# Block sums of the values on TensorE, and the low words of the weights rounded by ScalarE

## The chip, the core and the metric

One core of one Trainium2 chip runs the whole program. The engines named here are PE (TensorE, matrix multiply; PEld is its weight load), DVE (VectorE), ACT (ScalarE), POOL (GpSimd) and SP (SyncE, which issues every DMA of this kernel). The metric is the device time of one execution in microseconds (us); lower is better.

## The reference

A local-plus-summary attention over 2 batches, 8 heads, 768 positions and 64 channels is followed by two feed-forward layers on 1536 tokens of 512 channels. Weights and inputs of the layers arrive as float64, the attention's as float32.

```python
block, window = (32, 16)
nb = S // block                                   # 24 blocks
k_sum = k.reshape(B, H, nb, block, D).max(axis=3)
v_sum = v.reshape(B, H, nb, block, D).mean(axis=3)
scores_l = where(|i - j| < window, scale * q @ k.T, -1e9)
scores_s = scale * q @ k_sum.T + log(block)
a = softmax(concat([scores_l, scores_s]))
x = a @ concat([v, v_sum])                        # -> 1536 x 512
x = (x @ w_a) * (x @ w_b) @ w_out                 # d_ff = 1536
h = x @ w_in                                      # d_ff = 2048
return maximum(0.01 * h, h) @ w_out2
```

What matters here is `v_sum`, the mean of every 32 rows of v, and the conversion of the float64 weights.

## The kernel before

**Feed-forward part.** All products of the two layers run as three float32r matmuls of 512 columns (high times high, high times rest, rest times high; `mm3`, L578 to L582). A unit is a slice `s` of four hidden columns blocks and a chunk `c` of 512 tokens; `first_product` (L661) makes `x @ w_a` and `x @ w_b` into the PSUM banks a, b, c0, c1, `y_products` (L698) the product with `w_out`; the second layer follows at L783 to L798.

**Weights.** The chip has no float64, so each 128 x 512 piece arrives as pairs of 32-bit words (`wst`, two buffers) and is converted by seven steps in `convert` (L321): `low` (L335) scales the low word by 2^-29 and rounds it to an integer (DVE, L337) and takes the absolute value of the high word (ACT, L341); `clamp`, `shift`, `join` and `add` (L345 to L362, DVE) build the float32 bits; `high` (ACT, L367) and `rest_of` (DVE, L370) write the two parts in `wsp`, which the matmuls read. The buffer of the rounded low word, `wr`, is single. There are 68 such pieces in all. The steps stand in the list `bg`, from which `tick` takes a few after each product, so that they are spread between other work.

**Attention part.** `attention_ops` (L202) gives each step of the attention a place number: 8 per pair of blocks of 256 queries (`pairs`, twelve of them), plus an offset, and the list is sorted by it. The first four pairs run before the first unit of the feed-forward part, with the first matmuls of that part among them; the others are spread over the units (0, 0) and (0, 1) by `micro`. The steps share four PSUM banks t0 to t3 in turn (`at_bank`): keys are transposed and reduced by maximum (`k_prep`), queries transposed (`q_prep`), scores made in 64 x 64 quarters of the PE array (L515), masked and exponentiated (L528 on DVE, L532 on ACT), normalised, transposed, and multiplied with windows of v (`pv`, L562).

**Block sums of v.** Once for each batch `load_vb` (L149) brings v as three tiles `vb` of 128 half blocks x 16 rows x 64 channels. `v_sums` (L424) puts six DVE reductions (L428) at the head of `bg`: each sums the 16 rows of one tile for 32 channels. `v_place` (L440) then adds the two halves of every block, scales by 1/32 and moves each head's 24 blocks to partitions 0 to 23 by ten matmuls of 64 columns with the matrix `place` (L452); ACT copies the result (L459) and POOL spreads it over the windows (`put_sums`, L191).

The order on each engine's queue is worked out at compile time from the order of the code and a planner's estimate of the durations, so that instructions can stand elsewhere than the code has them.

Of the kernel before, what the change touches and what calls it, by code (L numbers as in the profile page):

```python
# [11 lines left out]
F32 = mybir.dt.float32  # L12
F32R = mybir.dt.float32r
I32 = mybir.dt.int32
U32 = mybir.dt.uint32
AF = mybir.ActivationFunctionType
ALU = mybir.AluOpType
AX = mybir.AxisListType
# [3 lines left out]
def kernel(  # L22
# [12 lines left out]
    nc = tc.nc  # L35
    B, H, S, D = q.shape
    P = 128
    BLK = 32
    WIN = 16
    NB = S // BLK  # L40
# [16 lines left out]
    T = 512  # L57
# [13 lines left out]
    const = ctx.enter_context(tc.tile_pool(name="const", bufs=1))  # L71
# [10 lines left out]
    sm_p = att.enter_context(tc.tile_pool(name="sm", bufs=4))  # L82
    at_p = att.enter_context(tc.tile_pool(name="at", bufs=2))

    def bank(tag):
        return psum.tile([P, T], F32, tag=tag, name=f"ps_{tag}")
# [5 lines left out]
    def at_bank():  # L92
        cnt["at"] += 1
        return bank(at_banks[cnt["at"] % len(at_banks)])
# [26 lines left out]
    NV = 2 * H * NB // P  # L121
    vb_tiles = [xp.tile([P, BLK // 2, D], F32, tag="x", name=f"vb{j}") for j in range(NV)]
    vs_t = {}
    bg, vb_done = [], [None]

    pace = {"micro": 0.0, "bg": 3, "after": None}
    q_t, k_t, vb_t, vw_of = {}, {}, {}, {}
# [19 lines left out]
        q_t[i] = t  # L147

    def load_vb(b):  # L149
        while vb_done[0] in bg:  # L150
            bg.pop(0)()
        src = v[b].rearrange("h (n j) d -> (h n) j d", j=BLK // 2)
        for i, t in enumerate(vb_tiles):
            nc.sync.dma_start(out=t, in_=src[i * P : (i + 1) * P])
# [43 lines left out]
    LOAD, SIDE, PRODUCT = range(3)  # L198
# [3 lines left out]
    def attention_ops():  # L202

        ops = []
        seen = set()
        for i, p in enumerate(sum(pairs, [])):

            def add(at, kind, f, *args):
                ops.append((PER * i + at, kind, lambda: f(*args), i))

            for m, (b, hp) in enumerate(dict.fromkeys(x[:2] for x in p)):
                if (b, hp) not in seen:
                    seen.add((b, hp))
                    add(-18, LOAD, load_k, b, hp)
                    for j in range(2):
                        add(2 * m + j - 12, PRODUCT, k_prep, b, hp, j)
                    if hp == 0:
                        add(-5, LOAD, load_vb, b)
                        add(-4, SIDE, v_sums, b)
                        add(7, PRODUCT, v_place, b)  # L220
            add(-14, LOAD, load_q, i, p)
            add(-6, PRODUCT, q_prep, i, p)
            for j in range(2):
                add(4 * j, PRODUCT, scores, i, p, j)
                add(4 * j + 3, SIDE, normal, i, j)
                add(4 * j + 8, PRODUCT, p_transpose, i, j)
            add(1, LOAD, load_vw, i, p)
            add(9, SIDE, put_sums, i, p)
            add(PV, PRODUCT, pv, i, p)
        ops.sort(key=lambda o: o[:2])  # L230
        return ops
# [5 lines left out]
    ident = const.tile([P, P], F32, tag="ident", name="ident")  # L237
# [9 lines left out]
    t = negm[1]  # L247
# [3 lines left out]
    for c in range(2):  # L251
        for o, c0, c1 in ((0, 0, W), (W, SC, P)):
# [3 lines left out]
                out=loc, in_=loc, compare_op=ALU.is_ge, fill=BIG,  # L256
# [3 lines left out]
                out=loc, in_=loc, compare_op=ALU.is_ge, fill=BIG,  # L260
# [4 lines left out]
        nc.vector.memset(negm[i][:, c0 : c0 + WIN], BIG)  # L265
    for t in vw_t:
        nc.gpsimd.memset(t, 0.0)

    V0 = 32
    place = const.tile([P, P], F32, tag="place", name="place")  # L270
    nc.gpsimd.memset(place, 1.0 / BLK)
    for base, pattern, mult in ((2 * V0, [[-2, P]], 1), (1 - 2 * V0, [[2, P]], -1)):

        nc.gpsimd.affine_select(
            out=place, in_=place, compare_op=ALU.is_ge, fill=0.0,
# [29 lines left out]
    def stage():  # L305
        key = pieces[cnt["st"]]
        cnt["st"] += 1
        nm, f = key
        t = wst_p.tile([P, 1024], I32, tag="wst", name="wst")
        if nm in "op":  # L310
            src = {"o": w_o, "p": w_o2}[nm][P * f : P * (f + 1), :]
            nc.sync.dma_start(out=t, in_=src)
        else:
            src = {"a": w_a, "b": w_b, "i": w_i}[nm][:, 2 * P * f : 2 * P * (f + 1)]
            nc.sync.dma_start(
                out=t.rearrange("p (k f) -> p k f", k=KT),
                in_=src.rearrange("(k p) f -> p k f", p=P),
            )
        staged[key] = t

    def convert():  # L321

        i = cnt["conv"]
        key = pieces[i]
        while cnt["st"] < min(i + 4, len(pieces)):
            stage()
        cnt["conv"] += 1
        ww = staged.pop(key).rearrange("p (f two) -> p f two", two=2)
        lo_w, hi_w = ww[:, :, 0], ww[:, :, 1]
        home = "early" if room["early"] else "late"  # L330
        assert room[home], key
        room[home] -= 1
        t = {}

        def low():  # L335
            t["r"] = wcv_p.tile([P, 512], I32, tag="wr", name="wr", bufs=1)
            nc.vector.tensor_scalar(  # L337
                out=t["r"], in0=lo_w.bitcast(U32), scalar1=2.0**-29, scalar2=None, op0=ALU.mult
            )
            t["c"] = wcv_p.tile([P, 512], I32, tag="wc", name="wc")  # L340
            nc.scalar.activation(out=t["c"].bitcast(F32), in_=hi_w.bitcast(F32), func=AF.Abs)  # L341

        def clamp():
            c = t["c"].bitcast(F32)
            nc.vector.tensor_scalar(  # L345
                out=c, in0=c, scalar1=F_LO, scalar2=F_HI, op0=ALU.max, op1=ALU.min
            )

        def shift():
            nc.vector.tensor_scalar(  # L350
                out=t["c"], in0=t["c"], scalar1=3, scalar2=0x3FFFFFF8,
                op0=ALU.logical_shift_left, op1=ALU.bitwise_and,
            )

        def join():
            nc.vector.scalar_tensor_tensor(  # L356
                out=t["c"], in0=hi_w, scalar=-0x40000000, in1=t["c"],
                op0=ALU.bitwise_and, op1=ALU.bitwise_or,
            )

        def add():
            nc.vector.tensor_tensor(out=t["c"], in0=t["c"], in1=t["r"], op=ALU.add)  # L362

        def high():
            pool = wsp_p if home == "early" else late["wsp"]
            t["w"] = pool.tile([P, 2, 512], F32R, tag="wsp", name="wsp")
            nc.scalar.copy(out=t["w"][:, 0], in_=t["c"].bitcast(F32))  # L367

        def rest_of():
            nc.vector.tensor_tensor(  # L370
                out=t["w"][:, 1], in0=t["c"].bitcast(F32), in1=t["w"][:, 0].bitcast(F32),
                op=ALU.subtract,
            )
            w_of[key] = t["w"], home

        bg.extend([low, clamp, shift, join, add, high, rest_of])

    def may_convert():
# [42 lines left out]
            xt[c, kt] = xp.tile([P, 2, T], F32R, tag="x", name=f"x{c}_{kt}")  # L421
        return xt[c, kt]

    def v_sums(b):  # L424

        v0 = sm_p.tile([P, NV, D], F32, tag="v0", name="v0", bufs=1)
        ops = [
            lambda i=i, d=d: nc.vector.tensor_reduce(  # L428
                out=v0[:, i, d : d + D // 2],
                in_=vb_tiles[i][:, :, d : d + D // 2].rearrange("p j d -> p d j"),  # L430
                op=ALU.add, axis=AX.X,
            )
            for i in range(NV)
            for d in (0, D // 2)
        ]
        bg[0:0] = ops
        vb_done[0] = ops[-1]
        vb_t[b] = v0, ops[-1]

    def v_place(b):  # L440

        v0, done = vb_t.pop(b)
        while done in bg:
            bg.pop(0)()
        ps = at_bank()
        for h in range(H):
            r0, r1 = 2 * h * NB, 2 * (h + 1) * NB
            tiles = range(r0 // P, (r1 - 1) // P + 1)
            for i in tiles:
                c0 = V0 + (r0 - i * P) // 2  # L450
                assert 0 <= c0 <= P - NB
                nc.tensor.matmul(  # L452
                    out=ps[0:NB, h * D : (h + 1) * D],
                    lhsT=place[:, c0 : c0 + NB],
                    rhs=v0[:, i],
                    start=i == tiles[0], stop=i == tiles[-1],
                )
        vs = sm_p.tile([NB, H, D], F32, tag="vs", name="vs", bufs=2)
        nc.scalar.copy(out=vs, in_=ps[0:NB].rearrange("p (h d) -> p h d", h=H))  # L459
        vs_t[b] = vs  # L460
# [167 lines left out]
    ops = attention_ops()  # L628
# [32 lines left out]
    def first_product(key, src, c):  # L661

        w = weights(key)
        ps = product_bank(key[0])
        for kt in range(KT):
            kt_mm(ps, w, src[c, kt], kt)
            if kt == KT // 2 - 1:
                interleave()
        return ps
# [114 lines left out]
    for f, c in slices2:  # L784
        ps = first_product(("i", f), ysp, c)
        h = g_p.tile([P, T], F32, tag="g", name="h")
        nc.scalar.copy(out=h, in_=ps)  # L787
        nc.vector.scalar_tensor_tensor(  # L788
            out=h, in0=h, scalar=0.01, in1=ps, op0=ALU.mult, op1=ALU.max
# [41 lines left out]
```

## Time and profile before

| | us |
|---|---|
| median of three runs (lowest, highest) | 661.57 (661.22, 662.78) |
| the profiled execution, own time | 661.62 |
| its span on the core | 659.9 |
| PE busy in the span | 635.6 (96%) |
| DVE busy | 422.0 (64%) |
| ACT busy | 267.8 (41%) |

The span runs from the first to the last instruction that the profiler saw; 1.7 us of the profiled execution lie around it. Busy shares are averages over stages with different limits, and the ends of matmuls are modelled, so a PE that is shown busy is not always a PE at its peak. The page also cuts the span in 40 slices of 16.5 us and gives the clock that was granted to PE in each.

### The profile page before, as it was taken

To read this page: it belongs to the slowest core of one execution; us is meant where nothing else is said; L and a number is where in the kernel's file an instruction comes from. 1 tells how busy PE (TensorE), PEld (TensorE's weight loads), DVE (VectorE), ACT (ScalarE), POOL (GpSimd) and SP (SyncE) were. 2 spreads that over 40 slices of the span, in tenths; PEclk is the share of its full clock that TensorE was granted. 3 is DMA by queue.
4 is the path that set the end of the run, shared out by engine and by line. 5 is a ranking of instruction groups with operands and counts; after the bars stand their busy time and mean duration, and the time that the engine had idled before them with its cause. 6 is when DMAs were issued, how large, how long until landed. Compare 5 with 4: busy or idle time off the path is not lost.

```text
span 659.9 us, 9321 instructions
## 1 busy us (share of the span) xinstructions
PE 635.6 (96%) x3448; PEld 518.4 (79%) x3448; DVE 422.0 (64%) x968; ACT 267.8 (41%) x607; POOL 21.1 (3%) x38
## 2 busy tenths in 40 slices
PE   5699799999999999999999999999999999999997
PEld 4567577777888888888888888888888888888886
DVE  5989999955999972699623779732279532422323
ACT  4677386653445421344222535322255322222221
POOL 3210020000000000000000000000000000000000
PEclk9899799999999999999999999999999999999999
DMA  9976543512334430143200232400014000100101
GB/s 239 258 174 162 148 107 109 151 26 65 125 130 133 156 96 1 64 125 121 74 1 0 67 93 77 147 1 1 0 51 141 1 0 1 64 1 1 64 1 64
DMA packets 72590, 53.43 MB, mean 81 GB/s; under 512 B 46176, under 2 KB 66656, under 8 KB 72544
## 3 DMA queue, kind: packets, MB, share of 16 engines
q1 hardware_dynamic: 72544, 52.84, 27.0%
q8 instruction: 27, 0.44, 0.3%
q14 instruction: 19, 0.16, 0.1%
HBM read 49.68 MB, written 3.15 MB: 80 GB/s over the span
## 4 chain that ended last, share of the span: by engine, by line
PE 89%; DVE 7%; ACT 2%; DMA 1%; issue 1%; SPq 0%; DVEq 0%; ACTq 0%
PE ps_t L580 38%; PE ps_c L580 19%; PE ps_a L580 14%; PE ps_b L580 13%; PE ps_t L515 2%; DVE pm L528 1%; PE ps_t L550 1%; PE ps_t L562 1%; ACT pm L532 1%; DVE v L428 1%; DVE pm L542 1%; DMA wst<-in_moe_w_b_dram 1%; DVE wc L356 1%; PE ps_t L497 1%; DVE wr L337 0%
## 5 line engine op out<-in xcount | busy, mean ns | idle before, releaser
L580 PE MATMUL ps_t<-x,wsp 128*128 128x512 f32 x336 | 78.6, 389 | 0.0
L580 PE MATMUL ps_c<-wsp,gs 128*128 128x512 f32 x288 | 75.8, 389 | 0.0
L580 PE MATMUL ps_t<-wsp,gs 128*128 128x512 f32 x288 | 74.7, 389 | 0.0
L580 PEld LDWEIGHTS ps_t<-x,wsp 128*128 128x128 f32 x336 | 63.1, 188 | 13.1
L580 PE MATMUL ps_t<-ys,wsp 128*128 128x512 f32 x288 | 71.9, 389 | 0.0
L580 PE MATMUL ps_a<-x,wsp 128*128 128x512 f32 x252 | 68.6, 410 | 3.0 <-DVE wsp L370 2.7
L341 ACT ACTIVATE wc<-wst 128x512 f32<-128x512 f32 x68 | 45.6, 673 | 55.3 <-DMA wst<-in_moe_w_out_dram 12.1
L580 PE MATMUL ps_b<-x,wsp 128*128 128x512 f32 x252 | 64.3, 394 | 0.5 <-DVE wsp L370 0.5
L580 PEld LDWEIGHTS ps_t<-ys,wsp 128*128 128x128 f32 x288 | 54.1, 188 | 11.2
L580 PEld LDWEIGHTS ps_c<-wsp,gs 128*128 128x128 f32 x288 | 54.0, 188 | 11.2
L580 PEld LDWEIGHTS ps_t<-wsp,gs 128*128 128x128 f32 x288 | 54.0, 188 | 11.2
L580 PE MATMUL ps_c<-gs,wsp 128*128 128x512 f32 x240 | 60.8, 394 | 0.0
L580 PEld LDWEIGHTS ps_a<-x,wsp 128*128 128x128 f32 x252 | 47.9, 194 | 14.2 <-DVE wsp L370 3.1
L788 DVE SCALAR_TENSOR_TENSOR h<-h,ps_t 128x512 f32<-128x512 f32 x24 | 16.5, 686 | 60.8 <-ACT h L787 60.8
L580 PEld LDWEIGHTS ps_b<-x,wsp 128*128 128x128 f32 x252 | 46.6, 188 | 10.6 <-DVE wsp L370 1.0
L370 DVE TENSOR_TENSOR wsp<-wc,wsp 128x512 fp32r<-128x512 f32 x68 | 47.2, 696 | 9.9 <-ACT wsp L367 9.8
L580 PEld LDWEIGHTS ps_c<-gs,wsp 128*128 128x128 f32 x240 | 44.4, 188 | 9.5 <-ACT x L572 0.2
L367 ACT CAST wsp<-wc 128x512 fp32r<-128x512 f32 x68 | 42.1, 622 | 19.6 <-DVE wc L362 13.8
L580 PE MATMUL ps_t<-gs,wsp 128*128 128x512 f32 x192 | 47.7, 390 | 0.0
L601 DVE TENSOR_TENSOR gs<-h,gs 128x512 fp32r<-128x512 f32 x48 | 33.1, 691 | 22.8 <-ACT gs L600 22.7
L362 DVE CUSTOM_DVE_ANT_0 wc<-wc,wr 128x1024 uint16<-128x1024 uint16 x68 | 46.6, 685 | 0.6
L356 DVE SCALAR_TENSOR_TENSOR wc<-wst,wc 128x512 int32<-128x512 int32 x68 | 46.7, 689 | 0.2
(86 smaller groups left out, 835.9 us busy)
## 6 DMA issues: line engine op xcount, KB each, us to landing
wst<-in_moe_w_out_dram SPq DMA_DIRECT2D x28, 512.0 KB, 3.3
wst<-in_moe_w_in_dram SPq DMA_DIRECT2D x16, 512.0 KB, 3.7
wst<-in_moe_w_a_dram SPq DMA_DIRECT2D x12, 512.0 KB, 3.6
wst<-in_moe_w_b_dram SPq DMA_DIRECT2D x12, 512.0 KB, 3.6
k<-in_k_dram SPq DMA_DIRECT2D x16, 192.0 KB, 3.5
vb<-in_v_dram SPq DMA_DIRECT2D x6, 512.0 KB, 5.3
out_dram<-acc SPq DMA_DIRECT2D x12, 256.0 KB, 2.1
q<-in_q_dram SPq DMA_DIRECT2D x16, 128.0 KB, 2.9
```

Source lines behind the costliest of these rows:

```text
L341: nc.scalar.activation(out=t["c"].bitcast(F32), in_=hi_w.bitcast(F32), func=AF.Abs)
L356: nc.vector.scalar_tensor_tensor(out=t["c"], in0=hi_w, scalar=-0x40000000, in1=t["c"], op0=ALU.bitwise_and, op1=ALU.bitwise_or,)
L362: nc.vector.tensor_tensor(out=t["c"], in0=t["c"], in1=t["r"], op=ALU.add)
L367: nc.scalar.copy(out=t["w"][:, 0], in_=t["c"].bitcast(F32))
L370: nc.vector.tensor_tensor(out=t["w"][:, 1], in0=t["c"].bitcast(F32), in1=t["w"][:, 0].bitcast(F32), op=ALU.subtract,)
L428: lambda i=i, d=d: nc.vector.tensor_reduce(out=v0[:, i, d : d + D // 2], in_=vb_tiles[i][:, :, d : d + D // 2].rearrange("p j d -> p d j") ...
L497: nc.tensor.transpose(ps[:, n * P : (n + 1) * P], q2[:, n].rearrange("p c d -> p (c d)"), ident)
L515: nc.tensor.matmul(out=ps[h, w, :], lhsT=qt[h, w * W : (w + 1) * W], rhs=kts[h, (g * G + w) * SC : (g * G + w) * SC + P], start=True, stop ...
L528: pace["after"] = nc.vector.tensor_tensor_reduce(out=pm[:, w, :], in0=ps[:, w, :], in1=m, scale=1.0, scalar=3.0e38, op0=ALU.add, op1=ALU.m ...
L580: nc.tensor.matmul(out=ps, lhsT=w(a), rhs=x(b), start=first and j == 0, stop=last and j == 2)
L601: nc.vector.tensor_tensor(out=t[:, 1], in0=src, in1=t[:, 0].bitcast(F32), op=ALU.subtract)
L788: nc.vector.scalar_tensor_tensor(out=h, in0=h, scalar=0.01, in1=ps, op0=ALU.mult, op1=ALU.max)
```

## The change

The block sums move from DVE to PE, with the halves added and the scaling done in the same matmuls. For each batch there are two calls of `v_sums`, each for four heads. Head `h` of the four writes to partitions 32 h to 32 h + 31 of one PSUM bank: `place` (32 of its columns) is the weight, and eight rows of 64 channels of a `vb` tile are the 512 moving columns. A head whose half blocks lie in one tile takes two such matmuls, one whose half blocks lie in two tiles takes four; the matmuls of the four heads are written in turn. One DVE reduction per call then adds the eight groups of 64 columns. `v_place` only moves heads to partitions 0 to 23, with slices of the identity, in eight matmuls of 64 columns instead of ten. The sums are no longer in `bg`, `load_vb` no longer empties `bg`, and the place numbers of `v_sums` go from -4 (six reductions in `bg`) to 1 and 2 (as products). Apart from this, `low` rounds the low words by an ACT instruction in place of the DVE one, and a constant `eps` is written once by POOL and read by nothing.

```diff
     def load_vb(b):
-        while vb_done[0] in bg:
-            bg.pop(0)()
         src = v[b].rearrange("h (n j) d -> (h n) j d", j=BLK // 2)
...
                     if hp == 0:
                         add(-5, LOAD, load_vb, b)
-                        add(-4, SIDE, v_sums, b)
+                        for j in range(2):
+                            add(1 + j, PRODUCT, v_sums, b, j)
                         add(7, PRODUCT, v_place, b)
...
+    eps = const.tile([P, 1], F32, tag="eps", name="eps")
+    nc.gpsimd.memset(eps, 1.0e-9)
...
         def low():
             t["r"] = wcv_p.tile([P, 512], I32, tag="wr", name="wr", bufs=1)
-            nc.vector.tensor_scalar(
-                out=t["r"], in0=lo_w.bitcast(U32), scalar1=2.0**-29, scalar2=None, op0=ALU.mult
+            nc.scalar.activation(
+                out=t["r"], in_=lo_w.bitcast(U32), func=AF.Copy, scale=2.0**-29
             )
...
-    def v_sums(b):
-
-        v0 = sm_p.tile([P, NV, D], F32, tag="v0", name="v0", bufs=1)
-        ops = [
-            lambda i=i, d=d: nc.vector.tensor_reduce(
-                out=v0[:, i, d : d + D // 2],
-                in_=vb_tiles[i][:, :, d : d + D // 2].rearrange("p j d -> p d j"),
-                op=ALU.add, axis=AX.X,
-            )
-            for i in range(NV)
-            for d in (0, D // 2)
-        ]
-        bg[0:0] = ops
+    HQ = P // V0
+
+    def v_sums(b, j):
+
+        ps = at_bank()
+        n = T // D
+        parts = []
+        for h in range(j * HQ, (j + 1) * HQ):
+            r0, r1 = 2 * h * NB, 2 * (h + 1) * NB
+            parts.append(
+                [
+                    (i, V0 + (r0 - i * P) // 2, j0)
+                    for i in range(r0 // P, (r1 - 1) // P + 1)
+                    for j0 in range(0, BLK // 2, n)
+                ]
+            )
+        for m in range(max(len(x) for x in parts)):
+            for h, x in enumerate(parts):
+                if m < len(x):
+                    i, c0, j0 = x[m]
+                    nc.tensor.matmul(
+                        out=ps[h * V0 : (h + 1) * V0],
+                        lhsT=place[:, c0 : c0 + V0],
+                        rhs=vb_tiles[i][:, j0 : j0 + n].rearrange("p j d -> p (j d)"),
+                        start=m == 0, stop=m == len(x) - 1,
+                    )
+        if j == 0:
+            vb_t[b] = sm_p.tile([P, H // HQ, D], F32, tag="v0", name="v0", bufs=1)
+        nc.vector.tensor_reduce(
+            out=vb_t[b][:, j], in_=ps.rearrange("p (j d) -> p d j", d=D), op=ALU.add, axis=AX.X
+        )
 
     def v_place(b):
...
         for h in range(H):
-            r0, r1 = 2 * h * NB, 2 * (h + 1) * NB
-            tiles = range(r0 // P, (r1 - 1) // P + 1)
-            for i in tiles:
...
+            j, r = divmod(h, HQ)
+            nc.tensor.matmul(
+                out=ps[0:NB, h * D : (h + 1) * D],
+                lhsT=ident[:, r * V0 : r * V0 + NB],
+                rhs=v0[:, j],
+                start=True, stop=True,
+            )
```

## Rows read from the trace of the kernel before

**Rows 1.** The page: busy tenths of 40 slices of 16.5 us, and the clock

```profile
PE   5699799999999999999999999999999999999997
DVE  5989999955999972699623779732279532422323
ACT  4677386653445421344222535322255322222221
PEclk9899799999999999999999999999999999999999
```

**Rows 2.** Busy time by stretch: PE, PEld, DVE, ACT, POOL, PE clock, DMA share, GB/s

```profile
0.00:16.50 16.50, 9.12 (x68) 7.56 (x68) 9.22 (x45) 7.52 (x28) 5.24 (x22) 1.00 0.91 239
16.50:33.00 16.50, 11.06 (x125) 8.97 (x127) 16.47 (x47) 10.86 (x35) 3.97 (x3) 0.90 0.93 258
33.00:49.50 16.50, 14.90 (x183) 11.26 (x180) 14.27 (x65) 13.18 (x50) 2.74 (x3) 1.00 0.71 174
49.50:66.00 16.50, 16.34 (x164) 13.05 (x162) 15.10 (x47) 12.74 (x41) 1.17 (x2) 1.00 0.66 162
66.00:82.50 16.50, 11.71 (x68) 8.69 (x68) 15.48 (x38) 6.52 (x21) 0.00 (x0) 0.79 0.57 147
82.50:99.00 16.50, 15.36 (x177) 12.14 (x176) 15.47 (x60) 14.16 (x49) 3.88 (x5) 1.00 0.41 107
...
181.50:198.00 16.50, 16.50 (x75) 13.65 (x74) 15.86 (x33) 7.77 (x13) 0.00 (x0) 1.00 0.39 130
```

**Rows 3.** The chain that ended last, first 100 us: start, us, what

```profile
11.65 0.78 DVE v L428
...
15.44 1.12 DVE v L428 x2
...
17.23 1.94 DVE v L428 x2
...
21.11 0.62 DVE wr L337
...
35.27 2.88 ACT pm L532 x15
...
70.08 0.61 DVE wsp L370
```

**Rows 4.** Groups of instructions by form: count, busy us, mean ns, idle before

```profile
L341 ACT ACTIVATE wc<-wst 128x512 f32<-128x512 f32 x68 | 45.6, 673 | 55.3 <-DMA wst<-in_moe_w_out_dram 12.1 <-DMA wst<-in_moe_w_in_dram 10.2 <-DVE wsp L370 10.2
...
L337 DVE TENSOR_SCALAR wr<-wst 128x512 int32<-128x512 uint32 x68 | 30.6, 450 | 1.7 <-DMA wst<-in_moe_w_a_dram 1.0 <-DMA wst<-in_moe_w_in_dram 0.5
...
L428 DVE TENSOR_REDUCE v<-vb 128x32 f32<-128x512 f32 x12 | 11.7, 1019 | 0.0
...
L479 DVE TENSOR_REDUCE ks<-ps_t 128x16 f32<-128x512 f32 x8 | 5.4, 681 | 0.0
```

**Rows 5.** PE in order of time, 65 to 83 us: start, us, idle before

```profile
67.40 0.63 PE L469 MATMUL ps_t<-ident,k 128*128 128x128 f32 x4 [1.48 <-issue]
70.74 4.64 PE L580 MATMUL ps_a<-x,wsp 128*128 128x512 f32 x10 [2.71 <-DVE wsp L370]
...
79.80 2.58 PE L580 MATMUL ps_b<-x,wsp 128*128 128x512 f32 x10
```

**Rows 6.** DVE in order of time, 65 to 95 us

```profile
65.44 0.42 DVE L337 TENSOR_SCALAR wr<-wst 128x512 int32<-128x512 uint32 x1
...
67.22 2.87 DVE L428 TENSOR_REDUCE v<-vb 128x32 f32<-128x512 f32 x3
70.01 0.68 DVE L370 TENSOR_TENSOR wsp<-wc,wsp 128x512 fp32r<-128x512 f32 x1
70.61 1.99 DVE L428 TENSOR_REDUCE v<-vb 128x32 f32<-128x512 f32 x2
```

**Rows 7.** The chain, later: PE pieces of few-column matmuls

```profile
78.68 1.19 PE ps_t L452 x18
...
82.38 0.24 PE ps_t L452 x2
...
104.07 1.08 PE ps_t L562 x32
105.15 0.58 PE ps_t L515 x8
...
109.79 1.02 PE ps_t L515 x16
...
111.47 0.38 PE ps_t L562 x8
```

**Rows 8.** Busy time around the stall, columns as in Rows 2

```profile
70.70:76.00 5.30, 5.26 (x18) 3.88 (x20) 5.30 (x10) 1.27 (x3) 0.00 (x0) 0.51 0.63 163
```

More of the change, by code (lines that the diff above doesn't have):

```diff
@@ L123 @@
     vs_t = {}
-    bg, vb_done = [], [None]
+    bg = []
     pace = {"micro": 0.0, "bg": 3, "after": None}
@@ L215, in attention_ops @@
                     for j in range(2):
-                        add(2 * m + j - 12, PRODUCT, k_prep, b, hp, j)
+                        add(2 * m + j + -12, PRODUCT, k_prep, b, hp, j)
                     if hp == 0:
                         add(-5, LOAD, load_vb, b)
-                        add(-4, SIDE, v_sums, b)
+                        for j in range(2):
+                            add(1 + j, PRODUCT, v_sums, b, j)
                         add(7, PRODUCT, v_place, b)
@@ L422, in x_tile @@
         return xt[c, kt]
-    def v_sums(b):
-        v0 = sm_p.tile([P, NV, D], F32, tag="v0", name="v0", bufs=1)
-        ops = [
-            lambda i=i, d=d: nc.vector.tensor_reduce(
-                out=v0[:, i, d : d + D // 2],
-                in_=vb_tiles[i][:, :, d : d + D // 2].rearrange("p j d -> p d j"),
-                op=ALU.add, axis=AX.X,
-            )
-            for i in range(NV)
-            for d in (0, D // 2)
-        ]
-        bg[0:0] = ops
-        vb_done[0] = ops[-1]
-        vb_t[b] = v0, ops[-1]
+    HQ = P // V0
@@ L440, in v_place @@
     def v_place(b):
-        v0, done = vb_t.pop(b)
-        while done in bg:
-            bg.pop(0)()
+        v0 = vb_t.pop(b)
         ps = at_bank()
         for h in range(H):
-            r0, r1 = 2 * h * NB, 2 * (h + 1) * NB
-            tiles = range(r0 // P, (r1 - 1) // P + 1)
-            for i in tiles:
[L450 to L456, printed above, removed]
-                )
+            j, r = divmod(h, HQ)
[5 more added lines that the diff above has]
+            )
```

## The prediction, made before the changed kernel was run

> **What bounds the kernel now.** I read the page's slices first. From slice 6 on PE stands at 9 tenths or more with its clock at full speed, but for the last slice; in the first five it is at 5, 6, 9, 9 and 7 [rows 1]. In the feed-forward stages a stretch of 16.5 us holds 75 matmuls of 512 columns, 220 ns each, without a pause [rows 2]. So the end of the kernel is the PE work that is left at about 84 us plus the time at which PE becomes continuously busy; DVE or ACT time saved after that point is worth nothing, although most of the 68 weight conversions lie there.
>
> Then the table by stretch: up to 82.5 us PE is busy 63.1 us and idle 19.4, of which 12.8 are in the first 33 us, while DVE is busy 14.3 to 16.5 of every 16.5 us from 16.5 us on [rows 2]. The front is therefore bound by DVE and by the order around it. The chain says which DVE work: the reductions of v at L428 stand on it with 0.78, 1.12 and 1.94 us between 11.6 and 19.2 us, and one rounding (L337) with 0.62 [rows 3]. Between 35 and 38 us ACT's exponentials are the chain [rows 3].
>
> Last the stall. PE waits 1.48 us and then 2.71 us for the part `wsp` of a weight that DVE writes at 70.01, and DVE does three L428 reductions (2.87 us, those of the second batch) directly ahead of that write and two more (1.99 us) behind it [rows 5, 6]. After the stall the granted clock is 0.51 from 70.7 to 76 us, the lower of the two levels, and ten matmuls take 4.64 us where ten others take 2.58 a little later [rows 5, 8].
>
> **The change, part by part.**
>
> Reductions off DVE. Twelve L428 of 1.02 us, 11.7 us, go; four reductions of 128 x 512 from PSUM come. Their price is bounded by L479 (0.68, from PSUM, elements in order) and L428 (1.02, the same crosswise reading) [rows 4]; I take 1.02 for the reading order, so DVE gets back 11.7 - 4.1 = 7.6 us, half of it for each batch. Each new reduction also holds one of the four shared banks until it is done.
>
> Sums onto PE. For each batch there are two calls of ten matmuls with 512 float32 columns. The trace has none of that width in full float32, so I price it from slopes. L515 pieces of 8 and 16 records take 0.58 and 1.02 us: eight records are four matmuls of 128 columns, two side by side, so one round of 128 columns costs 0.22 us and one of 512 columns 0.88; the remaining 0.14 us is what entering a batch costs [rows 7]. L562 (two groups of columns) gives 0.70 us for 24 records of 64 columns, 0.117 a round, 0.93 for 512. L452, where all matmuls write the same partitions, gives 0.95 us for 16 records, 0.119 for each single matmul of 64 columns [rows 7]. So L562 does two matmuls in the time in which L452 does one: column groups do run side by side, two of them. Four are not in the trace. Bounds for a batch of v: four side by side need four rounds per call, eight rounds, 7.0 us; two side by side need twelve rounds, 10.6 us; one at a time twenty, 17.6 us. I take four, since the pairs of L562 show no loss, and the heads are written in turn; with 0.1 us for entering, 7.1 us a batch. `v_place` saves two matmuls of 0.12 us a batch, under 0.3, so I leave it out.
>
> A rule speaks against that value. The row shows two groups at the full double rate [rows 7]. The Trainium skill, page "TensorE: Matmul & The Clock Gate", section "Measured speedup vs the span model", lists three column tiles of 512 columns at a speedup of 2.38 rather than 3. By my estimate from that page four would then cost 9.0 us a batch and the sum below would be 1.9 us higher for the second batch; the pairs in this trace do not agree with such a loss, and no row shows more than pairs.
>
> First batch (places 1 and 2, about 11 to 20 us): 7.1 us of PE work enter a stretch with 12.8 us of idle PE, of which 4.5 are the first load and cannot be filled. Some 8 us are left as cover, so I cost the matmuls at nothing. DVE's 3.8 us of L428 leave the chain there, but PE then has 7.1 us to do in the same place, ahead of the next scores, so I credit nothing either: 0, with -4 (all of it gained) and +4 (scores queue behind the sums, and DVE behind the scores) as bounds. DMA is at 0.91 and 0.93 in both first stretches [rows 2], which speaks against the whole gain.
>
> The rounding moved to ACT. Six L337 lie before the stall, from 21.03 to 65.44, one of them on the chain with 0.62. ACT's price is not in the trace; the nearest row is L341, which reads the same strided words, 0.67 us, against 0.45 on DVE [rows 4]. ACT is busy 44.3 of the first 66 us, so most of it is hidden in ACT's idle time; where ACT is the chain (35.27) one piece costs 0.67. I count DVE's gain on the chain as two steps of 0.62 and 0.4 us [rows 3, 6] and the loss as 0.67: -0.4. Bounds: -2 (six steps of some 0.33 us off DVE) and +4 (six times 0.67 on the chain). After 84 us PE hides both.
>
> Second batch, the stall: without the 2.87 us ahead of the write at 70.01, PE's 4.19 us of waiting shrink by 2.9. If PE no longer falls idle so long, the slow ten matmuls take 2.58 instead of 4.64: -2.1. Together -5.0 (bounds -1 and -6.3). The reductions behind the write delay the next weight too, but PE has other work by then: -0.5.
>
> Second batch, the matmuls: places 49 and 50 put them behind the first scores of the second batch, at 75 us or later, where PE is busy almost all the time: +7.1, nothing hides them.
>
> The list `load_vb` and `eps` cost nothing: the first only took reductions out of a list, and POOL is idle at the place of the second.
>
> Sum: 0 - 0.4 - 5.0 - 0.5 + 7.1 = +1.2 us on the profiled 661.6 (span 659.9 and 1.7 around it; the median of the runs is 661.57, the same to 0.05). Rounded down a little for DVE slack that I left out: **662.5 us**, no change that a measurement could tell, which I put at 0.3%, 2 us.
>
> **The rivals.**
>
> - *Balance* (the forecast): PE work added behind 75 us and the stall removed cancel. 662.5, own range 659 to 665.5. Chance 0.42.
> - *DVE's relief reaches further* (the other side): the 3.8 us of L428 on the chain before 20 us come out in full, because PE's sums fit into its idle time without delaying a score, and the weights stand ready about 4 us earlier. 662.5 - 4 - 1 = 657.5. For it: DVE is on the chain almost without a break from 10 to 28 us. Against it: DMA at over 0.9 and PE ahead of DVE in the same stretch. It decides from the point where PE is idle more than 7 us between 11 and 28 us. Chance 0.24.
> - *Two side by side*, or the planner spreads the matmuls of the four heads between others: 10.6 instead of 7.1 us a batch, +3.5 for the second and some +2 for the first: 668. Chance 0.16.
> - *No overlap*, the matmuls do not do what they are arranged for: 17.6 us a batch, +10.5 for the second and 10.5 less 2 of idle PE for the first: 662.5 + 19 = 681.5. Chance 0.08.
> - *ACT becomes the front's bound*: the roundings stand in ACT's queue ahead of exponentials, six times 0.67 us on the chain: 662.5 + 4 = 666.5. ACT's 13.18 busy of 16.5 us between 33 and 49.5 speaks for it [rows 2]. Chance 0.10. The Trainium skill, page "ScalarE: Activation LUTs", section "Rules for kernel authors", says to multiply on VectorE rather than ScalarE; rows 4 agree in duration (0.45 against 0.67 for the nearest ACT row), and by that rule this rival would be the likelier one.
>
> **How the numbers follow.** Faster by over 0.3%: all of the second case and 0.08 of the first, 0.32. Within: 0.26 of the first, 0.26. Slower: 0.08 of the first and the three others, 0.42. The range leaves out the case without overlap and the lower edge of the second: 655 to 676.
>
> **What would show it.** The new matmuls, grouped by line: a call of 20 records in about 3.6 us is four at a time, 5.3 two, 8.8 none. PE's idle time up to 82.5 us should fall from 19.4 to about 9, and the stretch after the first weight wait of the feed-forward part should run at full clock. ACT's rounding should take near 0.67 us. The stages after 165 us should be shifted, not changed. The prediction is wrong if the sums split up among other matmuls, if scores wait for a bank that a sum holds, or if the planner's new order opens a stall elsewhere in the front.

## The result, and the profile after

The changed kernel takes 668.71 us (median of 4 runs, 667.34 to 670.43) against 662.17 us (661.22 to 663.04) before on the same chips: a ratio of 1.0100, 95% interval 1.0085 to 1.0114. It is 6.5 us slower. The forecast was 662.5; the time lies beyond the own range of the likeliest case (659 to 665.5). It is inside the stated range by luck: that range reaches so far because of the rival with two matmuls side by side (668), to which the time is nearest and which the trace below rules out. Next comes the rival in which ACT holds up the front (666.5).

The page of the changed kernel, slices of 16.5 us, to be laid beside [rows 1]:

```profile
PE   6887999999999999999999999999999999999997
DVE  3976868955699962579542769732268532322323
ACT  4776857854567731355421547422256422222221
PEclk9889999999999999999999999999999999999999
```

DVE is relieved in the front, as it should be, but PE's hole has only moved: from the fifth slice to the third and fourth. The table by stretch (columns as in [rows 2]) says the same in numbers:

```profile
0.00:16.50 16.50, 10.99 (x74) 6.73 (x78) 6.51 (x41) 7.01 (x26) 5.26 (x23) 1.00 1.05 235
16.50:33.00 16.50, 14.24 (x152) 10.17 (x146) 15.24 (x43) 11.75 (x37) 3.24 (x3) 0.90 0.99 248
33.00:49.50 16.50, 13.63 (x150) 10.69 (x149) 12.71 (x54) 12.59 (x44) 1.42 (x2) 0.90 0.83 204
49.50:66.00 16.50, 11.82 (x108) 9.05 (x107) 11.26 (x36) 10.82 (x34) 3.01 (x4) 0.97 0.67 172
66.00:82.50 16.50, 16.50 (x129) 13.44 (x128) 14.42 (x47) 13.53 (x46) 0.00 (x0) 0.93 0.48 111
```

Up to 82.5 us DVE works 60.1 us instead of 70.5 and PE is idle 15.3 us instead of 19.4, although it has 6.4 us of sums more to do; the forecast had wanted about 9. The clock is below its upper level in four of these stretches (0.90, 0.90, 0.97, 0.93), where before it was in two (0.90, 0.79). Weighed by their length the shortfall is the same, 5.0 us against 5.1, so the 2.1 us that the forecast gained from the clock did not come in sum.

The groups by form price the new instructions (count, busy us, mean ns, idle before):

```profile
L338 ACT ACTIVATE wr<-wst 128x512 int32<-128x512 uint32 x68 | 45.9, 676 | 18.1 <-DVE wc L363 10.1 <-DMA wst<-in_moe_w_a_dram 6.7 <-DMA wst<-in_moe_w_in_dram 1.2
...
L453 DVE TENSOR_REDUCE v<-ps_t 128x64 f32<-128x512 f32 x4 | 2.8, 692 | 2.7 <-PE ps_t L445 2.7
```

The rounding costs 0.676 us on ACT (0.67 was taken) and the reduction from PSUM 0.69 (1.02 was taken). The 10.1 us for which the roundings wait on DVE's add (L363) all lie behind 157 us, where PE is busy without a pause. PE in order of time, with the idle time before each piece:

```profile
11.24 1.93 PE L445 MATMUL ps_t<-vb,place 128*32 128x512 f32 x6
13.10 1.36 PE L526 MATMUL ps_t<-kts,qt 64*64 64x128 f32 x16
14.40 4.54 PE L445 MATMUL ps_t<-vb,place 128*32 128x512 f32 x34
...
39.70 0.93 PE L508 MATMUL ps_t<-ident,q 128*128 128x128 f32 x4 [2.77 <-DMA q<-in_q_dram]
...
63.77 0.44 PE L480 MATMUL ps_t<-ident,k 128*128 128x128 f32 x2 [2.58 <-DVE ks L490]
65.37 0.79 PE L591 MATMUL ps_a<-x,wsp 128*128 128x512 f32 x1 [1.17 <-ACT x L583]
...
85.25 1.05 PE L445 MATMUL ps_t<-vb,place 128*32 128x512 f32 x2
...
86.81 5.39 PE L445 MATMUL ps_t<-vb,place 128*32 128x512 f32 x38
```

A batch of sums takes 6.4 us of PE for 40 records (20 matmuls, where one after the other was priced at 17.6 and two at a time at 10.6): the four heads do run side by side. The second batch stands at 85 to 92 us, where PE has no idle time left. Between 36 and 65 us there are new waits: for a load of q, then for DVE's maximum behind an ACT copy, then for ACT. The chain for that last one (start, us, what):

```profile
49.64 0.57 ACT wr L338
50.20 0.21 ACT wc L342
50.42 4.46 DMA wst<-in_moe_w_b_dram
54.96 0.66 ACT wc L342
55.62 1.16 ACT pm L543 x6
56.78 0.56 ACT wsp L368
57.34 0.60 ACT wr L338
57.96 3.75 DMA wst<-in_moe_w_a_dram
61.80 0.66 ACT wc L342
62.46 0.36 ACT kts L485
62.99 0.52 ACT wsp L368
63.51 0.57 ACT wr L338
64.08 0.77 ACT pm L543 x4
64.85 0.48 ACT x L583
65.37 0.79 PE ps_a L591
```

From 49.6 to 65.4 us the chain is drawn over ACT and the loads of weights, with three roundings (L338, 0.57 to 0.60 us each) on it. Before, it went in this stretch over PE (to 52.5 us), then ACT and one weight load (3.69 us from 55.63), then DVE. The links from ACT to a load, at 50.42 and 57.96, are inferred, and they don't hold: the staging buffers that these two loads fill had last been read at 44.7 and 54.1 us (DVE, L357), and SyncE was issuing other loads, one behind the other, until 50.3 and 57.9 us. What stands behind the largest wait, the 2.58 us at 63.77, is this:

```profile
51.47 6.38 SPq L175 DMA_DIRECT2D vw<-in_v_dram  x11
57.96 0.39 SPq L316 DMA_DIRECT2D wst<-in_moe_w_a_dram  x1
...
61.80 0.66 ACT L342 ACTIVATE wc<-wst 128x512 f32<-128x512 f32 x1 [3.40 <-DMA wst<-in_moe_w_a_dram]
...
63.02 0.69 DVE L490 TENSOR_REDUCE ks<-ps_t 128x16 f32<-128x512 f32 x1 [2.56 <-ACT kts L487]
```

The load of a weight was issued behind eleven loads of windows of v. ACT stood idle 3.40 us for it; the copies of k next in its queue, whose transposes PE had done by 61.2 us, came only then, DVE's maximum waited for them, and PE for the maximum. The step for which ACT waited is the absolute value, which it did before the change as well. Of the three roundings only the last (63.51) stands directly ahead of work that PE then waits for. So this trace does not show how the roundings cost time; that they do is shown by the runs below.

How far PE had come at a given time can be read from the records. In the fence each matmul record that both kernels have is weighed by its steady spacing (0.227 us for the 512-column ones, 0.0545 for scores, 0.029 for the products with v, 0.109 for transposes); the sums themselves and their placing are left out. A row gives the time at which so much common work had been started before, and how much later each kernel was. The last three columns are experiments told of below. Each column is one profiled execution: that of the sums alone took 664.65 us and its median is 663.73, so its last row reads 3.0 where the medians differ by 1.8. Beside a wait a row moves with the record at which it is taken, at 30 us by up to 1.2 us.

```
common work   before   changed   sums alone   first batch   second batch
14 us          35.50     +0.68        +3.97         +4.22          +1.54
30 us          56.25     +3.11        +4.45         +4.86          +1.51
35 us          61.39    +10.03        +7.29         +7.55          +1.50
45 us          81.75     +0.32        -1.64         +2.47          -0.89
60 us         100.37     +7.20        +4.09         +5.67          +3.08
100 us        146.32     +6.04        +3.01         +5.96          +2.00
```

At 82 us the changed kernel is where the old one was (+0.32). The forecast had it 5.9 us ahead there (0.4, 5.0 and 0.5). The sums alone are 1.6 us ahead, where the terms without the rounding had 5.5. Then the second batch comes, and 6 us are lost for good. From 146 us on nothing changes any more.

### The profile page after: what moved, and what is told of

It reads as the page before. It is cut to its first block, busy times and chain, and to the rows that moved or that the text cites. A ratio compares the mean times of both kernels' runs of the same rounds, so it can differ in the third digit from the quotient of the medians.

```text
span 665.9 us, 9482 instructions
## 1 busy us (share of the span) xinstructions
PE 646.9 (97%) x3520; PEld 522.2 (78%) x3520; DVE 395.8 (59%) x892; ACT 305.7 (46%) x675; POOL 19.9 (3%) x39
## 4 chain that ended last, share of the span: by engine, by line
PE 91%; DMA 3%; SPq 2%; ACT 2%; DVE 1%; issue 1%; ACTq 0%
PE ps_t L591 37%; PE ps_c L591 18%; PE ps_a L591 14%; PE ps_b L591 14%; PE ps_t L526 3%; PE ps_t L573 2%; PE ps_t L561 1%; DMA wst<-in_moe_w_a_dram 1%; PE ps_t L445 1%; DMA q<-in_q_dram 1%; SPq L175 1%; DMA wst<-in_moe_w_b_dram 1%; PE ps_t L508 1%; ACT pm L543 1%; SPq L132 1%
## 5 line engine op out<-in xcount | busy, mean ns | idle before, releaser
L591 PE MATMUL ps_a<-x,wsp 128*128 128x512 f32 x252 | 66.2, 400 | 1.2 <-ACT x L583 1.2
L591 PE MATMUL ps_b<-x,wsp 128*128 128x512 f32 x252 | 65.8, 396 | 0.0
L591 PEld LDWEIGHTS ps_t<-ys,wsp 128*128 128x128 f32 x288 | 54.1, 188 | 11.2
L338 ACT ACTIVATE wr<-wst 128x512 int32<-128x512 uint32 x68 | 45.9, 676 | 18.1 <-DVE wc L363 10.1
L799 DVE SCALAR_TENSOR_TENSOR h<-h,ps_t 128x512 f32<-128x512 f32 x24 | 16.5, 687 | 60.4 <-ACT h L798 60.4
L591 PEld LDWEIGHTS ps_c<-gs,wsp 128*128 128x128 f32 x240 | 44.7, 188 | 9.6 <-issue 0.3
L363 DVE CUSTOM_DVE_ANT_0 wc<-wc,wr 128x1024 uint16<-128x1024 uint16 x68 | 46.8, 688 | 2.1
L357 DVE SCALAR_TENSOR_TENSOR wc<-wst,wc 128x512 int32<-128x512 int32 x68 | 47.5, 702 | 0.6
```

The lines of the kernel that those rows point to most:

```text
L338: nc.scalar.activation(out=t["r"], in_=lo_w.bitcast(U32), func=AF.Copy, scale=2.0**-29)
L357: nc.vector.scalar_tensor_tensor(out=t["c"], in0=hi_w, scalar=-0x40000000, in1=t["c"], op0=ALU.bitwise_and, op1=ALU.bitwise_or,)
L591: nc.tensor.matmul(out=ps, lhsT=w(a), rhs=x(b), start=first and j == 0, stop=last and j == 2)
L799: nc.vector.scalar_tensor_tensor(out=h, in0=h, scalar=0.01, in1=ps, op0=ALU.mult, op1=ALU.max)
```

## The experiments

All were timed in rounds with the kernel before on the same chip, whose medians were 661.93, 662.37 and 662.57 us in the three groups of four. The intervals of the ratios are about 1 to 2 us wide to either side, so differences between two experiments are known to some 1.5 to 2 us.

**The sums alone.** The rounding is put back on VectorE in the changed kernel.

```diff
-            nc.scalar.activation(
-                out=t["r"], in_=lo_w.bitcast(U32), func=AF.Copy, scale=2.0**-29
-            )
+            nc.vector.tensor_scalar(
+                out=t["r"], in0=lo_w.bitcast(U32), scalar1=2.0**-29, scalar2=None, op0=ALU.mult
+            )
```

> The changed kernel with the rounding of the low words back on VectorE: only the block sums are moved. Theory A (the 6 us are the second batch's sums, which stand where TensorE is busy without a pause, and relief of VectorE or ScalarE in the front is worth nothing): the same as the changed kernel, 667 to 670 us. Rival B (the roundings in ScalarE's queue hold up the front and eat what VectorE gained): 663 to 665 us, and the stall near 60 us gone.

Measured: 663.73 us, ratio 1.0022 (1.0009 to 1.0035). Theory A falls: the sums, with all their PE work, cost 1.8 us, and the other 5.0 of the loss come with the rounding on top of them. Of B's signs the time is right; the stall near 60 us is smaller but not gone, as the table shows.

**The rounding alone**, the same edit the other way round in the kernel before.

> The kernel before with only the rounding of the low words moved to ScalarE. Theory A: no change, 661 to 664 us. Rival B: 665 to 667 us, the loss of the whole change without its matmuls.

Measured: 663.72 us, ratio 1.0022 (1.0003 to 1.0041), inside the range of theory A, though the interval speaks for a loss. The single runs reach from 661.98 to 667.81, and the profiled execution is the slowest of them, so its trace isn't read here. Alone the rounding costs 1.8 us, on top of the sums 5.0.

**The second batch earlier.** Place numbers 36 and 37 instead of 49 and 50, and the load earlier too.

```diff
-                        add(-5, LOAD, load_vb, b)
+                        add(-5 if b == 0 else -22, LOAD, load_vb, b)
                         for j in range(2):
-                            add(1 + j, PRODUCT, v_sums, b, j)
+                            add(1 + j - (0 if b == 0 else 13), PRODUCT, v_sums, b, j)
```

> The changed kernel with the second batch's sums 13 places earlier (36 and 37 instead of 49 and 50) and the load of its values 17 places earlier, so that the sums stand among the first four pairs, where TensorE has idle time. Theory A: the 6.3 us are hidden, 661 to 664 us. If the sums cost their time wherever they stand, 667 to 670 us. Rival B says nothing of where the sums stand: its stall would remain, and 6 us with it.

Measured: 668.13 us, ratio 1.0082 (1.0059 to 1.0105): the same as the changed kernel within what can be told. The sums stood where they were meant to:

```profile
53.83 3.63 PE L445 MATMUL ps_t<-vb,place 128*32 128x512 f32 x20
...
65.49 3.63 PE L445 MATMUL ps_t<-vb,place 128*32 128x512 f32 x20 [1.08 <-DVE ks L490]
```

By the time alone the run doesn't tell the last two expectations apart: rival B, with the rounding still on ACT, has the same range. By the measure of the table, though, this kernel is 4.6 us late at 45 us of common work, where the changed one is 0.3 late, and 6.4 late at 100, where the changed one is 6.0: the loss only comes earlier, and PE's idle time in the front did not hide it. A reading of this, argued and not shown: the idle time is waiting of an engine that works in order, the matmuls were done in one piece, and what stood behind them came later.

**The second batch's matmuls twice**, with the same result.

```diff
+        for _ in range(2 if b == 1 else 1):
+            for m in range(max(len(x) for x in parts)):
...
```

> The changed kernel with the matmuls of the second batch's sums made twice (same result). Theory A: 40 records more at the measured 6.3 us per 40, all on the path: +6.3, 674 to 676 us. If they are partly hidden: 669 to 672 us.

Measured: 676.16 us, ratio 1.0207 (1.0181 to 1.0232), 7.5 us over the changed kernel. In its trace the second lot of 40 records takes 12.26 - 5.39 = 6.9 us:

```profile
88.63 12.26 PE L446 MATMUL ps_t<-vb,place 128*32 128x512 f32 x78
```

So matmuls at this place cost at least their full time. This part of theory A holds.

**Two buffers for the rounded word.**

```diff
-            t["r"] = wcv_p.tile([P, 512], I32, tag="wr", name="wr", bufs=1)
+            t["r"] = wcv_p.tile([P, 512], I32, tag="wr", name="wr", bufs=2)
```

> The changed kernel with two buffers for the rounded low word instead of one, so that a rounding in ScalarE's queue no longer waits for VectorE's add of the piece before. Theory C (the rounding costs 5 us on top of the sums because it waits in ScalarE's queue for that add, with exponentials, copies and the release of the staging buffer behind it): 663 to 665 us, as with the sums alone. Theory D (what costs is ScalarE's own time of 0.67 us per piece, ahead of other work): 667 to 670 us, as the changed kernel.

Measured: 666.42 us, ratio 1.0054 (1.0037 to 1.0072), between the theories: 2.3 of the 5.0 us come back. The single buffer does not show as a wait of ACT: in the changed kernel no rounding waits for DVE's add before 157 us. It shows in the order. The sixth piece has its absolute value at 54.96 and its rounding only at 57.24, 0.56 us after the add of the piece before has ended (56.68), with other work between. With two buffers the steps stand side by side:

```profile
56.63 0.68 ACT L338 ACTIVATE wr<-wst 128x512 int32<-128x512 uint32 x1 [1.97 <-DMA wst<-in_moe_w_b_dram]
57.20 0.65 ACT L342 ACTIVATE wc<-wst 128x512 f32<-128x512 f32 x1
```

**The ACT instruction for nobody.** The sums moved, the rounding on VectorE, and in addition:

```diff
+            idle = wcv_p.tile([P, 512], I32, tag="wd", name="wd", bufs=2)
+            nc.scalar.activation(
+                out=idle, in_=lo_w.bitcast(U32), func=AF.Copy, scale=2.0**-29
+            )
```

> The sums moved, the rounding on VectorE, and the same ScalarE instruction issued as well into a tile of its own (two buffers) that nobody reads: ScalarE's time without the wait for the add and without a reader. Theory C: 663 to 665 us. Theory D: 667 to 670 us.

Measured: 666.51 us, ratio 1.0068 (1.0043 to 1.0093), again between: 2.8 us over the sums alone. The extra instruction keeps the staging buffer until it has read it, as the true one does, but waits for no add. With the run before it: of the 5.0 us about 2.8 would be ACT's instruction itself, and about 2.3 the order that the single buffer forces. This split is argued. The two parts add up to the whole, but each is known to 1.5 to 2 us only, and this kernel keeps the rounding on VectorE as well.

**The rounding on VectorE for the first eight pieces, on ACT for sixty.**

```diff
+            if i >= 8:
                 nc.scalar.activation(...)
+            else:
+                nc.vector.tensor_scalar(...)
```

> The changed kernel with the rounding on VectorE for the first eight pieces (those of the front, up to about 80 us) and on ScalarE for the other sixty. Theories C and D both: the cost lies in the front, 663 to 665 us. If it lies in the stages behind the front: 667 to 670 us.

Measured: 664.49 us, ratio 1.0039 (1.0025 to 1.0053). 4.2 of the 5.0 us lie with the eight pieces of the front; the other sixty roundings cost 0.8 us, within the noise.

**The rounding on GpSimd.**

```diff
-            nc.scalar.activation(
-                out=t["r"], in_=lo_w.bitcast(U32), func=AF.Copy, scale=2.0**-29
-            )
+            nc.gpsimd.tensor_scalar(
+                out=t["r"], in0=lo_w.bitcast(U32), scalar1=2.0**-29, scalar2=None, op0=ALU.mult
+            )
```

> The changed kernel with the rounding on GpSimd, which has little to do, in place of ScalarE. If the front only needs VectorE and ScalarE relieved: 659 to 663 us. If the rounding is slow there (over 2 us) or takes VectorE's time while it runs, so that the weights come later: 666 us and more.

Measured: 669.05 us, ratio 1.0110 (1.0079 to 1.0140). An idle engine is not enough. The group by form has the price:

```profile
L338 POOL TENSOR_SCALAR wr<-wst 128x512 int32<-128x512 uint32 x68 | 111.2, 1635 | 363.7 <-DVE wc L363 320.2 <-DMA wst<-in_moe_w_a_dram 22.4 <-issue 13.8
```

1.64 us instead of 0.45 on DVE or 0.68 on ACT, under the 2 us that the expectation named, and 320.2 of the 363.7 us of idle time ahead of it end with DVE's add, which reads the single buffer. DVE's own steps are longer in this run, too: `shift` (L351) takes 0.553 us in the mean, against 0.441 in the changed kernel. Whether the loss comes from the price, the buffer or the slower steps wasn't separated.

**One batch on PE, the other on DVE**, rounding on VectorE in both. The code of both kernels is kept side by side.

```diff
+                        if b == 0:    # in the other run: b == 1
                             for j in range(2):
                                 add(1 + j, PRODUCT, v_sums, b, j)
+                        else:
+                            add(-4, SIDE, v_sums_dve, b)
```

> The rounding on VectorE, the sums of the first batch on TensorE and those of the second on VectorE as before. By the prediction's terms (first batch hidden, 0; second batch 7.1 less 5.5): 661 to 663 us. If the first batch's sums hold up the scores and cost the time: 664 to 666 us.

> The rounding on VectorE, the sums of the second batch on TensorE and those of the first on VectorE. By the prediction's terms: 663 to 665 us, the whole loss of the sums moved alone (663.7). If the loss is the first batch's: 661 to 663 us.

Measured: the first batch on PE 667.99 us, ratio 1.0084 (1.0064 to 1.0104); the second batch on PE 664.26 us, ratio 1.0031 (1.0020 to 1.0043). The second is as the terms said, 1.7 us over the kernel before. The first is not: it loses 5.4 us, more than either of its expectations had. Its trace is 4.2 to 4.9 us late from 35 to 56 us on (table above). The second batch's reductions on DVE, which before were parted by the write of a weight [rows 6], then stand on the chain as one block of six (L484, from 75.46 to 81.25), and PE waits 2.90 us for a weight behind them:

```profile
75.54 3.12 DVE v L484 x4
...
79.33 1.93 DVE v L484 x2
```

```profile
82.56 0.74 PE L636 MATMUL ps_a<-x,wsp 128*128 128x512 f32 x2 [2.90 <-ACT wsp L373]
```

So the 5.4 us are not the price of the first batch's sums alone. With this block the kernel is 2.5 us late at 82 us, where the one with both batches on PE is 1.6 us ahead; how much of the rest is the sums' wasn't separated.

With the second batch on PE that waiting and the fall of the clock are nearly gone:

```profile
69.14 0.63 PE L525 MATMUL ps_t<-ident,k 128*128 128x128 f32 x4 [1.28 <-issue]
69.69 2.60 PE L636 MATMUL ps_a<-x,wsp 128*128 128x512 f32 x10
...
74.89 3.63 PE L450 MATMUL ps_t<-vb,place 128*32 128x512 f32 x20
...
81.39 3.63 PE L450 MATMUL ps_t<-vb,place 128*32 128x512 f32 x20
```

The ten matmuls take 2.60 us, where they took 4.64 [rows 5]. The two calls stand apart here, and each takes 3.63 us.

**Three staging buffers for the weights**, with the sums moved and in the kernel before.

```diff
-    wst_p = ctx.enter_context(tc.tile_pool(name="wst", bufs=2))
+    wst_p = ctx.enter_context(tc.tile_pool(name="wst", bufs=3))
```

> The sums moved, the rounding on VectorE, and three staging buffers for the weights instead of two. If the front waits at its end for weights that are loaded late because no staging buffer is free: 658 to 661 us, below the kernel before. If the loads are late for their place in SyncE's queue, or VectorE is what is late: 663 to 665 us.

> The kernel before with three staging buffers, the control of the run with three: if the buffer is what the front lacks, it gains here too, 657 to 660 us; if not, 661 to 664 us.

Measured: 664.70 us, ratio 1.0035 (1.0020 to 1.0050), and 661.99 us, ratio 0.9998 (0.9985 to 1.0011). With the rounding on VectorE the staging buffer is not what the front lacks; three buffers with the rounding on ScalarE were not tried. No kernel tried here was faster than the one before.

## Why the prediction was right and wrong

- **What bounds the kernel.** Right: everything is decided before 146 us, and work on DVE or ACT behind the front is worth nothing (60 roundings moved cost 0.8 us).
- **The price of the matmuls.** Right: 3.6 us were given for a call with four side by side; 3.63 were measured for one alone, and 6.3 to 6.4 for the two of a batch, which overlap a little, against 7.1 in the sum. The rivals with two side by side (10.6 us a batch) or none (17.6) fall. The Trainium skill, page "TensorE: Matmul & The Clock Gate", section "Measured speedup vs the span model", would have given 9.0 us by the estimate that stood there; the rows don't agree with it.
- **The second batch.** Right as a whole: -5.0 and -0.5 for the stall and +7.1 for the matmuls were +1.6, and alone it costs 1.7 us. The stall shrank and the ten matmuls came back to 2.6 us, as said; the matmuls cost their full time where they stand (7.5 us for the doubled lot).
- **The first batch.** Right in what it came to, wrong in how. It was costed at nothing, hidden in 8 us of idle PE, with +4 as bound. With the second batch on PE it adds 0.1 us (1.8 for both, 1.7 for the second alone), less than can be told apart. But it is not hidden: the two kernels of the table with the rounding on VectorE and the first batch on PE are 4 to 5 us late by 35 to 56 us. The idle time was there, but as waiting inside a chain of scores, exponentials and transposes, and not as cover. The delay is given back between 61 and 82 us, where the kernel before waits for a weight; with the second batch left on DVE a stall behind its reductions stands there, and the loss is 5.4 us in all. Why the order falls out so is only argued from the table.
- **The rounding.** This is the term that failed. It was put at -0.4 us, with -2 and +4 as bounds, and measured +1.8 alone and +5.0 on top of the sums. Its duration was right to 1%. The step that failed is that most of it would be hidden in ACT's idle time: 4.2 of the 5.0 us fall to the first eight pieces, in the front. The effect of the single buffer `wr`, which orders a rounding behind DVE's add, had no term; two buffers give 2.3 us back. The way by which the rest costs time is open: the largest wait of the changed kernel near 60 us (2.58) runs over a late weight load, and only the smaller one behind it (1.17) over a rounding. Of the rivals, ACT as the front's bound, priced at +4 with a chance of 0.10, came nearest to what the runs show. The Trainium skill, page "ScalarE: Activation LUTs", section "Rules for kernel authors", was named there as speaking for it, and the runs agree with it: 0.676 us on ACT against 0.450 on DVE, and slower in both pairs of kernels that differ in it alone (1.8 and 5.0 us).
- **What it came to.** +1.6 for the sums and -0.4 for the rounding against +1.8 and +5.0: nearly the whole miss of 5 to 6 us is the rounding. That the sums came out within 0.2 us is in part luck: by the table the sums alone are 1.6 us ahead at 82 us, where their terms had 5.5, and lose 4.7 us from there, where the terms had 7.1. The signs named for the forecast (PE idle falling to 9 us, full clock behind the first weight wait) failed: 15.3 us and 0.93. Two signs of its being wrong came: the sums were split by other matmuls (6 and 34 records, 2 and 38), without a higher price, and the new order opened waits elsewhere in the front (2.77 and 2.58 us).
- **Open.** The order on every queue is worked out anew for each kernel, so a run that changes one part also moves other instructions. How much of the 2.8 us is the 0.67 us per piece, and how much what the planner does with it, wasn't separated. That the rounding alone costs 1.8 and with the sums 5.0 is likewise measured and not explained. The late weight load of the changed kernel stands behind other loads in SyncE's queue; what an earlier place for it would give with the rounding on ScalarE was not tried.

## What to carry to other kernels

Idle time of an in-order engine in a latency-bound stretch is no sure cover: 6.4 us of matmuls put into it made the front 4 to 5 us late, and whether that was given back hung on what came behind. Price a moved step at its place in the queue, by who stands behind it, before counting on holes. Relieving the busiest engine pays only if its work doesn't go to an engine that feeds the same chain: moving 0.45 us from VectorE to 0.68 on ScalarE, between the exponentials, cost more (5.0 us) than all the sums that the other half of the change moved (1.8). Split a change into its parts and time them apart: here the sum for one half came out within 0.2 us, in part by luck, and the other missed by 5.

## What the runs showed of the hardware

Four column groups of 32 ran side by side with 512 full float32 columns: a call that needs four rounds took 3.63 us, when four rounds at the slope of pairs were 3.52. A crosswise reduction of 512 elements per partition took 1.02 us from SBUF to 32 results [rows 4] and 0.69 from PSUM to 64. Rounding 512 strided 32-bit words per partition took 0.45 us on VectorE, 0.68 on ScalarE and 1.64 on GpSimd.
